# Regrouping V by TensorE for one more batch, and loading half of the first q through a second queue

## The chip, the cores and the metric

The kernel runs on one core of a Trainium2 chip. The core has a matrix engine (TensorE, PE in the profile; its weight loads are listed apart as PEld), a vector engine (VectorE, DVE), a scalar engine (ScalarE, ACT), GpSimd (POOL) and SyncE (SP), which here only issues DMAs. Each engine works through its own list of instructions in program order and waits on semaphores for the others. Matmuls write PSUM; VectorE and ScalarE copy the results out to SBUF. GpSimd's DMAs can change the type on the way (fp32 to bf16); SyncE's copy as it is.

The metric is device time in microseconds. Before the change it is 104.95 us (median of three runs, 104.95 to 105.63). The profiled execution has a span of 101.9 us from its first to its last instruction.

## The reference

Four batches, eight heads, 768 positions in eight blocks of 96, head size 64. The first half is an attention within blocks, whose keys and values are mixed over blocks by a Sinkhorn-normalized matrix P; the second half is a token mixer on the result.

```python
for _ in range(5):
    P = P - np.max(P, axis=-1, keepdims=True)
    P = np.exp(P)
    P = P / (np.sum(P, axis=-1, keepdims=True) + 1e-09)
    P = P / (np.sum(P, axis=-2, keepdims=True) + 1e-09)
k_sorted = np.einsum('bhij,bhjcd->bhicd', P, k_b)      # v_sorted likewise
scores = scale * np.matmul(q_b, k_sb.transpose(0, 1, 2, 4, 3))   # within each block of 96
attn = softmax(scores)
x = np.matmul(attn, v_sb)                    # then heads joined: (4, 768, 512)
wq = x @ w_q ; wk = x @ w_k                  # 64 columns each
W_tok = scale * np.einsum('bsd,btd->bst', wq, wk)
mixed = np.einsum('bst,btd->bsd', W_tok, x)
out = np.maximum(mixed, 0.0) @ w_out         # fp32, (4, 768, 512)
```

## The kernel before

Everything is unrolled. A string, ORDER, lists some 450 items; each has a letter for the step, a digit for the batch, a number for the part, and a last character: a PSUM bank for TensorE steps (capitals), or the engine (A ScalarE, D VectorE, P GpSimd, S SyncE) for the others. The program is written in that order, so every engine's own queue is the order of its items in the string; nothing reorders them.

The steps of a batch b:

- l: loads by GpSimd, with the cast to bf16: n = 0, 1, 2 is q, k, v of the batch (768 KB in bf16, 128 partitions by 8 heads by 6 rows by 64); l03 and l04 load the mixer's weights wqk and wo. The tiles Qn, Kn, Vn have three buffers each, so batch 3 takes those of batch 0.
- c: the Sinkhorn steps, small operations that alternate between ScalarE (Exp) and VectorE. b and B turn P and spread it to PSUM; n (VectorE for batch 0, GpSimd for the others) multiplies it by a mask into M, whose two buffers alternate by batch. i: constants (idb, the identity; zero and one fills). Z: filler matmuls on zeros while TensorE has nothing else.
- Q and q: TensorE transposes q, and the eviction writes QT. K and k: the matmul of Kn with M gives the mixed K, transposed, in KT.
- The values are needed as VT, with 96 positions of a block on partitions. There are two ways. One (F, f, A, a): the matmul of Vn with M as for K (F), an eviction to a spare tile (f), transposes on TensorE (A) and an eviction to VT (a), four parts each. The other (V, v, R): a matmul with M as the weights (V, three parts), an eviction to Vs (v), and six DMAs of 132 KB from Vs to VT that regroup partitions (R, on SyncE). Before the change batch 0 goes the first way and batches 1, 2 and 3 the second. For batch 1 there are also gates (N): GpSimd copies one element of Vs, so that later loads in its queue are not issued before the regrouping.
- S and e: scores and the Exp on ScalarE (E). P, r, x: attention times V with a row sum, reciprocal, and normalization on VectorE (X). T and t: transposes of X (XT).
- J, j, W, w, G, g, H, h: the mixer's projections and products (qkT, qD, wk, Ab, mixT), with d a copy of half of qkT to other partitions, by an engine or by a SyncE DMA. O and o: the product with wo and the eviction to ot; y: the store.

GpSimd's queue is in order: l00 l01 l02 i00 i02 l03 l11 l10 l12 n10 l04 n11 l20 n21 n20 n30, then gates N12 N11, l21, gates N12 N11 N10, l30 l22 l32 n31 l31. SyncE's begins with the load of sort_net into Pm and then has the six R of batch 1, y02, and the R of batches 2 and 3 with y00 and y01 among them, then the other stores.

The lines named in the profile are mostly those of helpers: L140 is every matmul, L144 the copy on ScalarE, L146 the copy on VectorE, L101 a load, L306 the regrouping, L322 a gate, L220 the product into M, L336 the Exp of the scores, L365 and L370 the normalization.

Of the kernel before, what the change touches and what calls it, by code (L numbers as in the profile page):

```python
# [8 lines left out]
FP32 = mybir.dt.float32  # L9
# [6 lines left out]


ORDER = """
l00P l01P l02P i00P i02P l03P c00D c01D i01D Z087 c02D i03A Z257 l11P c03D Z357 c04D Q007 Q016 l10P
Q025 c05D Z560 q02A q00A b00D B005 Z040 q01A n03D l12P n02D u00A K030 n01D n10P K022 n00D K016 l04P  # L20
k03D K004 k01A n11P k00D S050 S066 e05A k02D F014 e06A f01D F020 F032 f02A S006 f03D S014 l20P e00A
A021 F002 e01A a02D S036 n21P A010 f00D e03A S044 A031 a01D e04A n20P A007 a03D K112 a00A K104 k11D
P040 k10A P006 r04D K132 x04D P034 r00D k13A S020 x00D e02A K122 r03D Q127 x03D k12A Q116 P020 q11A
q12D T035 Q104 r02D t03A x02D P012 q10A r01D T025 x01D V120 S156 v12A t02D S122 T004 e15A T015 R14S
t00D V110 R15S t01D e12A V106 J005 n30P v10D v11A N12v N11v l21P N12v N11v N10v l30P l22P S132 l32P
J025 J014 e13A R13S j00D S110 n31P R11S J034 d00D R12S e11A W005 S102 j01D R10S S166 w00D e10A W014
d01D G005 Q221 w01A e16A S142 q22D G015 e14A Q210 g01D Q201 q21A H022 q20D H004 H016 h02A h01D l31P
h00A O043 O002 o04A O037 o00D K230 o03D K202 k23A K224 k20D P136 k22A S250 r13D S262 x13D e25A P124
e26A r12D S240 x12D P146 e24A Q303 Q312 r14D q30A x14D P110 q31D K214 T133 r11D k21A T122 x11D P106
t13A S214 t12D S220 e21A T113 r10D x10D O052 e22A V204 t11D o05A T107 v20D V220 y02S t10A V212 O016  # L30
v22A v21D R20S R21S J117 o01A R25S V320 R24S J137 R23S J106 v32D R22S j11A V302 y00S d11A W117 J126
v30A S204 R35S w11D j10D S230 R34S O027 e20A d10D R31S R30S W106 e23A V312 o02D Q325 w10D y01S v31A
K320 q32D K306 G104 k32D R32S k30A K332 R33S G114 k33D S300 g11A K316 e30A H124 k31D H112 h12A H100
h11D P226 h10A O155 r22D x22D S332 S320 O104 e33A o15A P246 P212 o10A r24D O145 x24D e32A r21D P206
x21D o14A S340 O114 y12S e34A r20D x20D T215 o11A P230 t21A S312 y10S r23D S356 T204 x23D e31A O135
e35A t20D P300 T224 o13A r30D T237 x30D t22A P312 P335 t23A J204 r31D r33D x31D J211 J224 O120 j20A
x33D d20S T304 o12A J231 W207 t30D P322 j21A y11S w20A S365 d21D W214 r32D e36A G207 x32D w21A P340
G217 r34D x34D T326 g21A T315 t32D T334 t31A H210 t33D H202 H226 h21D J305 h20A J314 h22A J325 O203
j30D J334 d30A W302 O225 o20A j31D w30D d31S G304 o22A W317 O216 w31A G314 o21A O235 g31D y20S H320
o23A H312 H306 O244 h31D y21S h30A O255 o24A O327 o25A h32D O314 y22S o32D O355 o31A y35S O337 y34S  # L40
o35A O344 y38S o33A O305 y36S o34A y37S o30A y33S
"""


# [1 line left out]
def kernel(  # L46
# [11 lines left out]
    nc = tc.nc  # L58
    B, H, S, D = q.shape
# [3 lines left out]
    P = 128  # L63
# [5 lines left out]
    DM = moe_w_out.shape[0]  # L69
# [16 lines left out]
    def tiles(name, n, shape, dtype=BF16):  # L86
        return [sb.tile(shape, dtype, name=f"{name}{i}") for i in range(n)]

    PS = psp.tile([P, 8, 512], FP32, name="ps")
# [6 lines left out]
    Qn, Kn, Vn = (tiles(n, NIN, [P, H, R6, D]) for n in ("Qn", "Kn", "Vn"))  # L96
# [3 lines left out]
    def load(t, src, b):  # L100
        nc.gpsimd.dma_start(out=t[b % NIN].rearrange("p h r d -> p h (r d)"),  # L101
                            in_=src[b].rearrange("h (p r) d -> p h (r d)", p=P))
# [12 lines left out]
    mixT = tiles("mixT", 1, [P, 2, 2, R6, P])  # L115
# [17 lines left out]
    def rows(t):  # L133
        return t.unsqueeze(2).to_broadcast([BH, NB, NB])

    def cols(t):
        return t.unsqueeze(1).to_broadcast([BH, NB, NB])
# [4 lines left out]
    def copy(e, o, i):  # L142
        if e == "A":
            nc.scalar.copy(o, i)  # L144
        else:
            nc.vector.tensor_copy(o, i)  # L146
# [2 lines left out]
        return PS[:, n, :].bitcast(BF16)  # L149


    def u_c(b, n, e):
        if n == 0:
            nc.vector.memset(Pm[:, NB:NB + 1, :], 1e-9)
            nc.vector.memset(fil, 0.0)
            nc.vector.memset(filw, 0.0)  # L156
            nc.vector.reduce_max(tmp, Pv, axis=AX.X)
            nc.vector.tensor_sub(Pv, Pv, rows(tmp))
            return
        nc.scalar.activation(Pv, Pv, ACT.Exp)  # L160
        nc.scalar.copy(filw[:, n, 0:1], fil[:, 0:1])
        nc.vector.reduce_sum(tmp, Pv, axis=AX.X)
        nc.vector.reciprocal(tmp, tmp)
        nc.vector.tensor_mul(Pv, Pv, rows(tmp))
        nc.vector.reduce_sum(tmp, Pm.rearrange("p i j -> p j i"), axis=AX.X)
        nc.vector.reciprocal(tmp, tmp)
        nc.vector.tensor_mul(Pb if n == 5 else Pv, Pv, cols(tmp))


    def u_i(b, n, e):  # L170
        if n == 0:
            nc.gpsimd.memset(idb, 0.0)
            nc.gpsimd.affine_select(out=idb, in_=idb, compare_op=ALU.not_equal, fill=1.0, base=0,
                                    pattern=[[-1, P]], channel_multiplier=1)
        elif n == 1:
            nc.vector.reduce_max(m_p, idb.rearrange("p (j s) -> p s j", s=SP), axis=AX.X)
        elif n == 3:
            nc.scalar.copy(Lx.rearrange("p i j s -> p (i j) s"),
                           idb[0:BH, 0:BH].unsqueeze(2).to_broadcast([BH, BH, SP]))
        elif n == 2:  # L180
            for t in VT:
                nc.gpsimd.memset(t.rearrange("p i (h e) -> p i h e", e=DS)[:, :, :, D:DS], 1.0)  # L182
            for t in Vs:
                nc.gpsimd.memset(t[:, :, :, D:DS], 1.0)
            for t in KT:
                nc.gpsimd.memset(t[:, :, S:S + P - BLK], 0.0)
            for t in E:
                nc.gpsimd.memset(t[:, :, 2 * TH * BLK:EW], 0.0)  # L188
                nc.gpsimd.memset(t[:, NT - 1, 2 * (NB * NP - TH * (NT - 1)) * BLK:EW], 0.0)  # L189


    def u_l(b, n, e):
        if n == 3:
            for s, w in enumerate((moe_w_q, moe_w_k)):
                nc.gpsimd.dma_start(out=wqk[:, :, s, :], in_=w.rearrange("(t p) d -> p t d", p=P))  # L195
        elif n == 4:
            nc.gpsimd.dma_start(out=wo, in_=moe_w_out.rearrange("(t p) d -> p t d", p=P))
        else:
            load((Qn, Kn, Vn)[n], (q, k, v)[n], b)

# [248 lines left out]
    def oslot(b, n):  # L449
        return ot[(b * 3 + n // 2) % NOT]  # L450

    def u_o(b, n, e, bank):
        copy(e, oslot(b, n)[:, n % 2, :], PS[:, bank, :])

    def u_y(b, n, e, bank=None):
        od = out[b].rearrange("(p r) e -> p r e", r=R6)
# [8 lines left out]
    for item in ORDER.split():  # L465
        kind, b, n, arg = item[0], int(item[1]), int(item[2:-1]), item[-1]
# [40 lines left out]
```

The softmax here doesn't subtract the row's maximum and nothing guards it: scores larger than these inputs give would overflow.

## Time and profile before

| | busy, us | share of 101.9 us |
|---|---|---|
| TensorE (PE) | 90.3 | 89% |
| weight loads (PEld) | 60.4 | 59% |
| VectorE (DVE) | 71.8 | 71% |
| ScalarE (ACT) | 73.8 | 72% |
| GpSimd (POOL) | 24.9 | 24% |
| GpSimd's DMA queue | 10.09 MB | 66.6% of 16 DMA engines |
| SyncE's DMA queue | 8.83 MB | 24.7% of 16 DMA engines |

A matmul is in the table from its start until its result is through the array, so TensorE can be shown busy while it could take more work. Busy shares are averages: the kernel has a start (Sinkhorn and first loads), a long middle and an end of products and stores, and each has its own limit. A row of groups gives the operation, what it writes and reads, the shape, the count, then busy time and the mean in ns of one, then the idle time of the engine just before it and what ended most of that. A wait is written as who waited, for whom, the total, the count and the longest.

### The profile page before, as it was taken

How to read it: one execution, taken by the hardware profiler on the slowest of the kernel's cores; microseconds unless marked ns; L12 is line 12 of the kernel's file. 1: busy time of each engine (PE TensorE's matmuls, PEld its weight loads, DVE VectorE, ACT ScalarE, POOL GpSimd, SP SyncE). 2: the span in 40 equal slices, each digit the busy share in tenths (PEclk: the TensorE clock that was granted, in tenths of full speed). 3: DMA queues.
4: the chain of work that ended last, by engine and by line, in shares of the span. 5: the costliest groups of instructions: out<-in, count | busy, mean ns of one | idle time of the engine just before them, and what ended most of it. 6: DMA issues, size and time to landing. Idle time of an engine off the chain costs nothing.

```text
span 101.9 us, 3431 instructions
## 1 busy us (share of the span) xinstructions
PE 90.3 (89%) x1468; PEld 60.4 (59%) x1468; DVE 71.8 (71%) x137; ACT 73.8 (72%) x108; POOL 24.9 (24%) x42
## 2 busy tenths in 40 slices
PE   3987897999988996968989998999999999999940
PEld 1235366888867584357968777656786865534410
DVE  3877689889994957359997777878889987046200
ACT  5231948998869999539898797979995669556650
POOL 5999459920000999100000000000000000000000
PEclk9999999999999999999999999999999999999998
DMA  0899999999999989999999999960630500055992
GB/s 3 86 205 203 203 204 187 202 210 198 204 208 204 239 118 216 237 206 203 205 204 203 253 335 315 337 214 0 278 140 0 225 6 0 19 206 206 370 344 109
DMA packets 19037, 19.12 MB, mean 188 GB/s; under 512 B 1872, under 2 KB 17104, under 8 KB 19024
## 3 DMA queue, kind: packets, MB, share of 16 engines
q0 software_dynamic: 14064, 10.09, 66.6%
q1 hardware_dynamic: 4960, 8.83, 24.7%
q8 instruction: 11, 0.18, 0.7%
q14 instruction: 2, 0.02, 0.0%
HBM read 20.19 MB, written 6.29 MB: 260 GB/s over the span
## 4 chain that ended last, share of the span: by engine, by line
DMA 43%; PE 35%; POOL 15%; issue 2%; POOLq 1%; ACT 1%
PE ps L140 35%; DMA Kn<-in_k_dram 21%; DMA Vn<-in_v_dram 19%; DMA VT<-Vs 3%; POOL Kn L101 3%; POOL Qn L101 3%; POOL M L220 2%; POOL Vn L101 2%; POOL wqk L195 1%; POOL E L189 1%; POOL gate L322 1%; POOLq L502 1%; ACT ot L144 1%; POOL E L188 0%; POOL VT L182 0%
## 5 line engine op out<-in xcount | busy, mean ns | idle before, releaser
L336 ACT ACTIVATE E<-ps 96x960 bf16<-96x960 f32 (+1 forms) x28 | 24.1, 900 | 1.8 <-PE ps L140 1.3
L140 PE MATMUL ps<-wo,mixT 128*128 128x512 bf16 x96 | 23.3, 380 | 0.9 <-ACT mixT L440 0.9
L370 DVE TENSOR_TENSOR X<-ps,R 96x896 bf16<-96x896 f32 (+1 forms) x20 | 20.0, 1003 | 0.6
L144 ACT COPY ot<-ps 128x512 f32<-128x512 f32 x20 | 11.6, 586 | 5.2 <-PE ps L140 4.6
L140 PEld LDWEIGHTS <-mixT 128*128 128x128 bf16 x96 | 8.4, 97 | 10.5 <-ACT mixT L440 1.8
L220 POOL TENSOR_TENSOR M<-PTR,m_p 128x512 bf16<-128x512 bf16 x6 | 7.9, 1316 | 14.7 <-PE ps L140 12.0
L140 PE MATMUL ps<-VT,E 96*128 96x65 bf16 x256 | 10.8, 193 | 0.1
L140 PE MATMUL ps<-fil,filw 128*128 128x512 bf16 x28 | 8.6, 455 | 2.4 <-DVE filw L156 1.6
L140 PEld LDWEIGHTS <-E 96*128 96x128 bf16 x256 | 9.3, 97 | 1.9 <-DMA VT<-Vs 0.2
L140 PE MATMUL ps<-QT,KT 64*128 64x96 bf16 x256 | 9.2, 204 | 1.0 <-ACT E L336 0.4
L144 ACT CAST KT<-ps 128x768 bf16<-128x768 f32 x8 | 6.3, 798 | 5.0 <-PE ps L140 4.9
L146 DVE CAST KT<-ps 128x768 bf16<-128x768 f32 x8 | 7.5, 954 | 2.0 <-PE ps L140 1.7
L140 PE MATMUL ps<-M,Kn 128*64 128x128 bf16 x192 | 7.4, 221 | 1.4 <-DMA Kn<-in_k_dram 1.2
L140 PEld LDWEIGHTS <-KT 64*128 64x128 bf16 x256 | 6.2, 94 | 3.4 <-issue 1.8
L140 PE MATMUL ps<-idb,X 96*128 96x96 bf16 x128 | 7.5, 206 | 0.3 <-issue 0.3
L140 PEld LDWEIGHTS <-Kn 128*64 128x64 bf16 x192 | 5.9, 109 | 3.1 <-DMA Kn<-in_k_dram 2.0
L442 DVE TENSOR_SCALAR mixT<-ps 128x1024 bf16<-128x1024 f32 x5 | 6.1, 1221 | 2.1 <-PE ps L140 2.0
L140 PEld LDWEIGHTS <-X 96*128 96x128 bf16 x128 | 6.0, 98 | 2.0 <-issue 0.9
L140 PE MATMUL ps<-idb,Qn 128*64 128x128 bf16 x192 | 6.6, 220 | 0.7 <-DMA Qn<-in_q_dram 0.7
L144 ACT COPY QT<-ps 128x1024 bf16<-128x1024 bf16 x7 | 6.9, 1009 | 0.4 <-PE ps L140 0.3
L440 ACT ACTIVATE mixT<-ps 128x1024 bf16<-128x1024 f32 x7 | 6.8, 1022 | 0.3 <-PE ps L140 0.2
L140 PE MATMUL ps<-XT,wqk 128*128 128x384 bf16 x32 | 6.9, 327 | 0.0
(75 smaller groups left out, 131.5 us busy)
## 6 DMA issues: line engine op xcount, KB each, us to landing
out_dram<-ot SPq DMA_DIRECT2D x9, 512.0 KB, 2.7
Qn<-in_q_dram POOLq DMA_DIRECT2D x4, 768.0 KB, 14.0
Kn<-in_k_dram POOLq DMA_DIRECT2D x4, 768.0 KB, 11.7
Vn<-in_v_dram POOLq DMA_DIRECT2D x4, 768.0 KB, 16.4
VT<-Vs SPq DMA_DIRECT2D x18, 132.0 KB, 4.8
out_dram<-ot SPq DMA_DIRECT2D x6, 256.0 KB, 2.1
wo<-in_moe_w_out_dram POOLq DMA_DIRECT2D x1, 512.0 KB, 17.1
qD<-qkT SPq DMA_DIRECT2D x2, 48.0 KB, 1.9
```

The lines of the kernel that those rows point to most:

```text
L101: nc.gpsimd.dma_start(out=t[b % NIN].rearrange("p h r d -> p h (r d)"), in_=src[b].rearrange("h (p r) d -> p h (r d)", p=P))
L140: nc.tensor.matmul(o, w, x, is_transpose=t, start=start, stop=stop, skip_group_check=True)
L144: nc.scalar.copy(o, i)
L146: nc.vector.tensor_copy(o, i)
L189: nc.gpsimd.memset(t[:, NT - 1, 2 * (NB * NP - TH * (NT - 1)) * BLK:EW], 0.0)
L195: nc.gpsimd.dma_start(out=wqk[:, :, s, :], in_=w.rearrange("(t p) d -> p t d", p=P))
L220: ENG[e].tensor_tensor(out=M[b % 2][:, h0:h1], in0=src.unsqueeze(2).to_broadcast([P, nh, SP, NB]), in1=m_p.unsqueeze(1).unsqueeze(3).to_br ...
L322: nc.gpsimd.tensor_copy(gate, src)
L336: nc.scalar.activation(E[b % 2][:, n, 0:2 * w * BLK].rearrange("p (t a c) -> p a t c", a=2, c=BLK), PS[0:BLK, bank:bank + 2, 0:w * BLK].re ...
L370: nc.vector.tensor_mul(xo.rearrange("p (a t d) -> p a t d", a=2, d=D), avps(bank, w)[:, :, :, 0:D], rr[b, n][:, :, 0:w].unsqueeze(3).to_br ...
L440: nc.scalar.activation(o, i, ACT.Relu)
L442: nc.vector.tensor_relu(o, i)
```

## The change

Batch 1's values go the first way too: four F, f, A, a instead of three V and v, six R and five gates. Its spare tile is mixT, which is unused at that time (batch 0 uses XT[1]). This takes regrouping DMAs away and puts matmuls and evictions in their place.

Half of the first q (four heads) is loaded by SyncE as fp32 into the same mixT, right after sort_net, and two copies on ScalarE (i04, i05) cast it into Qn; GpSimd loads the other half. An eviction of O can be split by columns over ScalarE and VectorE (engine letter B); only the very last one is.

ORDER was rewritten throughout. GpSimd's queue is now: l03, l00 (half), i00, l01, i02, l02, l12, l10, l11, l20, n10, n11, l04, l21, n21, n20, l32, l22, l31, l30, n30, n31. SyncE's is: sort_net, half of q, d00, d01, R32, R33, R20, R21, y00, R23, R22, d11, R24, R25, R35, R34, R31, y01, R30, y02, and the other stores. TensorE's, from its first Q to the first K of batch 2, is:

```
Q017 Q026 Z560 Q005 B004 Z040 K010 K022 K006 K034 S020 F002 S016 F024 F030 S042 S036 A025 A004
S050 S062 A035 F016 F110 S002 P034 A017 P040 A116 F102 P004 Q107 P020 T036 P012 A105 Q114 K136
K100 T025 T013 T002 K116 F130 Q125 J004 F122 S126 S110 A135 J024 A123 J012 S106 J032 W005 P110
S163 W012 P106 S154 G003 K120 G013 K214
```

Fillers go from 28 to 32. The code:

```diff
+    HQ = H // 2
+    stage = mixT[0].rearrange("p a c r s -> p (a c r s)").bitcast(FP32).rearrange("p (h e) -> p h e", h=HQ)
+    nc.sync.dma_start(out=stage, in_=q[0, 0:HQ].rearrange("h (p r) d -> p h (r d)", p=P))
...
+        elif n in (4, 5):
+            h = 2 * n - 8
+            copy(e, Qn[0][:, h:h + 2].rearrange("p h r d -> p h (r d)"), stage[:, h:h + 2])
...
+        elif b == 0 and n == 0:
+            nc.gpsimd.dma_start(out=Qn[0][:, HQ:H].rearrange("p h r d -> p h (r d)"),
+                                in_=q[0, HQ:H].rearrange("h (p r) d -> p h (r d)", p=P))
         else:
             load((Qn, Kn, Vn)[n], (q, k, v)[n], b)
...
-        copy(e, oslot(b, n)[:, n % 2, :], PS[:, bank, :])
+        c = 0 if e != "B" else DM // 2
+        if e == "B":
+            copy("A", oslot(b, n)[:, n % 2, 0:c], PS[:, bank, 0:c])
+        copy("D" if e == "B" else e, oslot(b, n)[:, n % 2, c:DM], PS[:, bank, c:DM])
```

More of the change, by code (lines that the diff above doesn't have):

```diff
@@ L18 @@
 ORDER = """
[L19 to L38, printed above, removed]
@@ L39 @@
-j30D J334 d30A W302 O225 o20A j31D w30D d31S G304 o22A W317 O216 w31A G314 o21A O235 g31D y20S H320
-o23A H312 H306 O244 h31D y21S h30A O255 o24A O327 o25A h32D O314 y22S o32D O355 o31A y35S O337 y34S
-o35A O344 y38S o33A O305 y36S o34A y37S o30A y33S
+l03P l00P i00P l01P i02P l02P c00D c01D i01D Z080 l12P c02D i03A Z250 l10P c03D Z350 i04A c04D Z440
+l11P i05A Q017 Q026 c05D Z560 Q005 q01A q02A b00D B004 Z040 q00A l20P n01D n02D u00A K010 n00D n10P
+K022 n03D K006 k01D k02A K034 n11P k00A k03D S020 F002 e02A S016 f00D l04P F024 e01A F030 f02D S042
@@ new lines @@
+S036 e04A f03D A025 A004 e03A a02D S050 S062 a00D A035 e05A l21P F016 a03D e06A F110 n21P f01A S002
+f11D P034 e00A A017 n20P r03D P040 x03D A116 a01A F102 r04D a11A P004 x04D l32P Q107 r00D f10A P020
+x00D q10A T036 P012 r02D A105 x02D t03A Q114 a10A K136 r01D K100 x01D k13A l22P T025 k10D q11A T013
+T002 K116 t02D t01A F130 t00D Q125 k11A J004 l31P q12D f13A F122 S126 f12A S110 A135 e12A J024 A123
+a13D J012 e11A j00D S106 a12D J032 d00S e10A W005 l30P P110 j01D S163 w00D d01S W012 r11D e16A P106
@@ new lines @@
+x11D w01A S154 G003 e15A r10D K120 x10D G013 n30P k12A K214 g01D Q212 k21A S130 q21D P146 n31P e13A
+T103 r14D S144 x14D Q202 e14A t10D H010 H006 q20D Q223 h01A h00D P124 q22A V310 r12D O022 v31D S226
+o02A O013 x12D e22A P130 o01D T112 R32S V204 r13D t11A R33S x13D V216 O003 v20A K230 v21A o00D R20S
+H024 R21S T132 k23D y00S h02A T123 R23S K206 R22S t13D K300 t12A k20D K334 O052 k30A k33D S210 o05A
+S256 S264 J113 e21A J102 e26A J133 V220 e25A j11D J122 V324 j10D d11S v22A W113 V306 w11D W102 v32A
@@ new lines @@
+O033 v30D R24S R25S S200 d10A R35S o03D K324 R34S e20A K316 R31S w10D Q313 k32D y01S k31A G102 R30S
+Q301 q31D G112 q30D Q320 g11A K224 q32D H112 k22A H106 O041 h11D h10A S234 o04D S242 e23A S316 O100
+y02S e24A P244 O131 r24D o10A x24D e31A P202 o13D S334 O110 r20D e33A x20D P216 o11A S364 H122 r21D
+O121 e36A y10S x21D h12A P234 o12A S346 r23D S302 O140 x23D e34A y11S e30A T201 o14D P224 S326 t20A
+r22D P302 x22D e32A T230 O151 r30D t23A x30D T227 o15A T216 P324 t22D y12S t21A S350 r32D P312 x32D
@@ L42 @@
+e35A J207 J216 r31D J227 x31D P340 J236 j20A P334 j21A W207 r34D d20A T313 r33D x34D W212 w20A T306
+w21A x33D G207 t30A G217 t31D T322 d21D g21A T333 t32A H200 t33D H214 H226 h20D J302 h21A J313 h22A
+J322 O225 j30D J333 d30A W302 O234 o22A j31D w30A d31A W313 G302 o23A w31D O205 y21S G312 o20A O213
+g31A H310 o21A H304 H326 h31D O252 h30A y20S O243 o25D O335 o24A h32D O322 y22S o33A O343 o32A y36S
+O357 y35S o34A O302 y37S o35A O313 y38S o30A y33S o31B y34S
 """
```

## The prediction

> **What bounds the kernel now.** The page came first, for the shares of the whole span:
>
> ```profile
> span 101.9 us, 3431 instructions
> PE 90.3 (89%) x1468; PEld 60.4 (59%) x1468; DVE 71.8 (71%) x137; ACT 73.8 (72%) x108; POOL 24.9 (24%) x42
> DMA  0899999999999989999999999960630500055992
> ```
>
> No single engine is it: TensorE looks full, DMA is full until about 65 us, VectorE and ScalarE are each over 70%. So the second view is the busy time by stage. I cut it at the first start of a few TensorE groups: K of batch 0 (13.4), V of batch 1 (29.7), K of batch 2 (44.35), K of batch 3 (61.75), the first O of batch 2 (84.7), the first O of batch 3 (92.7). The columns are length, then busy time of PE, PEld, DVE, ACT, POOL.
>
> ```profile
> 13.40:29.70 16.30, 14.73 (x369) 12.33 (x369) 14.77 (x23) 13.66 (x17) 6.92 (x6) 1.00 1.37 202
> 29.70:36.70 7.00, 6.70 (x118) 4.92 (x119) 5.09 (x10) 6.22 (x7) 3.42 (x8) 1.00 1.19 207
> 36.70:44.35 7.65, 5.98 (x91) 3.39 (x88) 4.42 (x6) 5.21 (x8) 4.47 (x5) 1.00 1.19 199
> 44.35:61.75 17.40, 16.48 (x333) 13.13 (x333) 13.97 (x23) 15.24 (x20) 0.00 (x0) 1.00 1.27 233
> 61.75:84.70 22.95, 22.76 (x399) 16.37 (x400) 19.82 (x31) 18.33 (x29) 0.00 (x0) 1.00 0.45 161
> 84.70:92.70 8.00, 8.00 (x59) 3.71 (x57) 2.96 (x5) 5.46 (x9) 0.00 (x0) 1.00 0.30 118
> ```
>
> Read the mean share of DVE and ACT: 87% in the first row (28.43 of 32.6), 63% in the third, 84% and 83% in the fourth and fifth. The PSUM evictions on these two pace the kernel as much as TensorE does, and the third row is a hole. The waits and the GpSimd timeline say why:
>
> ```profile
> POOL M L220 <- PE ps L140: 12.0, 1, 12.0
> ```
> ```profile
> 32.92 1.31 POOL L220 TENSOR_TENSOR M<-PTR,m_p 128x512 bf16<-128x512 bf16 x1 [12.00 <-PE ps L140]
> 34.64 0.94 POOL L101 DMA_DIRECT2D Kn<-in_k_dram  x1
> 44.34 1.03 PEld L140 LDWEIGHTS <-Kn 128*64 128x64 bf16 x36 [1.28 <-DMA Kn<-in_k_dram]
> ```
>
> GpSimd issues the loads in program order. It stands 12 us in n30, which overwrites the M that batch 1's V still reads, then in the gates for the regrouping; l21 (K of batch 2) is issued only at 34.6. The DMA engines run nearly dry at 37 us (37 GB/s in a quarter microsecond against a steady 203), and K of batch 2 is used at 44.35.
>
> For TensorE, busy time is too kind. I took the time from a group's first matmul to the next group's where nothing waits: O 0.865 (the last eight groups: 7.08 us), V 0.45, A 0.44, Q 0.46, G 0.44, P 0.425 (0.26 short), K and F 0.34, T 0.34, S 0.30 (0.18 short), J 0.49 and 0.165, H 0.22, W 0.21. The order's groups then sum to 73.4 us. From 44.35 to 84.7 they are 36.1 of 40.35 us (89.5%); from the first P of batch 2 (65.7) to 84.7, 17.9 of 19.0 (94%). So late in the kernel TensorE is near its issue limit.
>
> **What the Trainium skill says.** "Perfetto Trace Analysis", section "Identifying the Most-Contended Engine": matmul busy time is a poor measure, occupancy is fair for Vector and Scalar. The trace agrees: 89% busy, but 73.4 us of issue in 101.9. "DMA: Bandwidth & Descriptors", section "Issuing engines are not separate DMA queues": DMAs of all issuers share the same 16 engines, so moving half of q to SyncE saves issue time, not bandwidth; no run here shows it yet. "ScalarE: Activation LUTs", section "What ACT_TABLE_LOAD costs": neighbouring activations overlap by about 93 ns. The trace agrees: four E activations of 0.97 us take 3.55 us, 0.11 less each, so sums of row means overstate.
>
> **The change, part by part.**
> *V of batch 1.* Removed: three V groups (3 x 0.45 = 1.35 us of PE), three evictions to Vs (ACT 1.02 x 2, DVE 1.23: 3.26 us), six regrouping DMAs of 132 KB and the five gates. Added: four F (4 x 0.34) and four A (4 x 0.44), 3.1 us of PE; four f (ACT 0.80 x 3, DVE 0.95) and four a (ACT 1.01 x 2, DVE 0.69 x 2), 6.75 us. The rows of batch 0 show all of these:
>
> ```profile
> L144 ACT CAST Vs<-ps 128x1024 bf16<-128x1024 f32 x5 | 5.1, 1016 | 0.8 <-DVE X L370 0.8
> L146 DVE CAST Vs<-ps 128x1024 bf16<-128x1024 f32 x4 | 4.9, 1225 | 1.5 <-PE ps L140 1.2 <-ACT E L336 0.2
> L146 DVE CAST XT<-ps 128x768 bf16<-128x768 f32 x3 | 2.8, 946 | 0.0
> L146 DVE COPY VT<-ps 96x1024 bf16<-96x1024 bf16 x3 | 2.1, 685 | 0.3 <-ACT E L336 0.3
> L144 ACT COPY VT<-ps 96x1024 bf16<-96x1024 bf16 x1 | 1.0, 1012 | 0.0
> ```
>
> Net +1.8 us of PE and +3.5 us of eviction, 1.75 on each of ACT and DVE, on the pacing engines. The regrouping removed was 0.81 MB, some 2 us of DMA at some 400 GB/s (quarter microseconds of the regrouping and stores near 65 us show 377 to 431), and the latency from V to P (4.8 us to landing) that batch 1 no longer has.
>
> *First q by halves.* The DMA engines carry almost nothing before 4 us while GpSimd writes descriptors. SyncE, free after its 0.40 us issue of sort_net, can move 0.79 MB in this time: its fp32 half needs some 2 us at 400 GB/s, so it lands at about 5. GpSimd's stream loses 0.39 MB, 1.9 us at 203 GB/s; wqk, now ahead of it, costs 0.65 us by bytes, up to 1 for its small packets. i04 and i05 cast on ACT, 0.80 each by the 768-element rows. They add a wait in ACT's queue with the Sinkhorn Exps behind it; but i04 follows the fourth Exp (6.5) and i05 the fifth (8.3), and ACT idles 1.44 us before each later Exp. Cost nothing, hidden by DVE's Sinkhorn chain, which sets B at 12.1 and K at 13.4 as before.
>
> *Loads.* All gates go, and V1, Q1, K1, Q2, wo and K2 are queued before GpSimd waits for M of batch 0. The stream then runs without a hole at 3.87 us a load: K0 at about 11.3, V0 15.2, V1 19.0, Q1 22.9, K1 26.8, Q2 30.6, wo 33.2, K2 37.1, V3 41, V2 45, K3 48.7, Q3 52.6, the last ones up to 3 us later for stores and regrouping beside them. Before, K1 was used at 21.9, K2 at 44.35, K3 at 61.75. K1 is later, which is why F and A of batch 1 stand before it: they fill TensorE with V1.
>
> *The order.* Adding each list's evictions at the row means, the mean of ACT and DVE from the first K of batch 0 to the first K of batch 2 is 25.6 us in the old order (measured 24.7, ratio 0.965) and 23.9 in the new: 23.1. From there to the first O of batch 2 it is 36.4 old (measured 33.7, 0.926) and 39.8 new: 36.9. PE from K of batch 2 on: 36.1 old, 40.6 new, since more of batch 0 and 1 is left for later.
> First stretch at the density of the hole-free row: 23.1/0.872 = 26.5, so K of batch 2 at 39.9, after its data (37.1). Second stretch, with loads ahead of need and regrouping no longer just in time (in the chain that ended last, P of batch 2 waits 3.39 us for VT): PE at the 94% of the stretch from 65.7, 40.6/0.94 = 43.2; eviction is then at 85%, under the 87% already seen. The first O of batch 2 stands at 83.1 instead of 84.7. What follows is the same O chain (8.0 and 9.2 us). The last eviction, split over ACT and DVE, saves some 0.2 (0.59 to the 0.37 of a 256-column copy). Sum: 1.6 + 0.2 = 1.8; 104.95 - 1.8 is 103.1, and I say 103.0.
>
> *Small ones.* qD by SyncE for three halves: 1.9 us to landing against 0.26 on DVE, but H comes several groups later. SyncE's queue holds y00, waiting for an O eviction, ahead of R23, R22, d11 and the rest of R2; P of batch 2 and H of batch 1 wait for those and come 10 us of PE work later or more. l32 waits behind n20 for F of batch 0, about 21 us, with 15 us of loads still queued. Four more filler matmuls run in idle time. Cost of all: nothing.
>
> **The rivals.**
> *Denser:* without data waits, the first stretch reaches 92% and PE 96%: 13.4 + 25.1 + 42.3 = 80.8, 4.1 us gained, 100.8. For: the hole had 37% free. Against: no stretch shows 92%.
> *Eaten up:* the extra eviction and PE work take back what the hole gave: PE at 91%, 13.4 + 26.5 + 44.6 = 84.5, 104.7. For: 44.35 to 61.75 ran at 86% with loads mostly there.
> *Slower:* the hole was dependence (the H, relu, O chain, with 1.38 us waited on mixT), not loads, and comes back elsewhere: the whole stretch's 81.9% stays (116.7 of 142.6). Work 60.0/0.819 = 73.3, the O at 86.7, 2.0 later less 0.2: 106.8. For: ACT gets more than its half of the new work, and SyncE's queue can block. Against: batch 1 loses a DMA in its chain.
>
> **How the numbers follow.** Forecast 103.0: 0.45. Denser 0.25, eaten up 0.13, slower 0.17. The range takes in the denser case to just under its value and most of the slower side: 100.3 to 105.8. Below 103.9 lie the denser case and most of the forecast: 0.63. Within 1%: 0.19. Above 106.0: 0.18.
>
> **What would show it.** DMA at 203 GB/s without a dip from 4 to about 55 us; no GpSimd wait of 12 us; K of batch 2 used near 40, K of batch 3 near 50; ACT near 80 us and DVE near 72 busy; F and A of batch 1 between 19 and 28. Wrong would be the part on q if the first Q stays at 8.6 us with loads no earlier, or if ACT's Exps slip; wrong the part on density if DVE plus ACT stay under 82% from 13.4 on. A wait of PE on VT or qD of a microsecond would point to SyncE's queue.

## The result and the profile after

The changed kernel takes 104.62 us in the median (102.88 to 106.81) beside 104.95 for the kernel before. Some executions of each kernel run 1.5% or more above its fastest; the ratio compares only the others, and since the first profiled execution of the changed kernel was one of the long ones, the lines below are from a second profile of the same kernel, the run a_again. The ratio is 0.9875, 95% interval 0.9833 to 0.9918, that is 103.2 to 104.1 us on the old 104.95: a gain of 1.3 us, where the forecast of 103.0 had 1.95. In a_again the ratio is 0.9801 (0.9739 to 0.9863).

The page of the changed kernel, the lines that answer to those of before (the lines of its program have moved: L231 is the product into M, L317 the regrouping):

```profile
span 101.2 us, 3544 instructions
PE 91.7 (91%) x1528; PEld 62.1 (61%) x1528; DVE 71.5 (71%) x137; ACT 78.6 (78%) x115; POOL 23.9 (24%) x37
DMA  1899999999999999999999844952705000145992
```

The DMA line is now full from the third slice to 55 us without the dip at 37 us. ScalarE has 4.8 us more to do, TensorE 1.4 us. The stages, cut where the same groups start: K of batch 0 (13.72), K of batch 1 (28.83), K of batch 2 (39.56), K of batch 3 (52.37), the first O of batch 2 (84.0), the first O of batch 3 (91.82). Columns as before: length, then busy time of PE, PEld, DVE, ACT, POOL.

```profile
13.72:28.83 15.11, 13.38 (x337) 11.48 (x337) 13.42 (x21) 13.74 (x17) 10.38 (x10) 1.00 1.32 204
28.83:39.56 10.73, 10.56 (x232) 8.57 (x232) 7.86 (x14) 9.40 (x13) 1.64 (x2) 1.00 1.30 205
39.56:52.37 12.81, 11.70 (x224) 8.36 (x226) 10.24 (x17) 9.95 (x13) 0.97 (x1) 1.00 1.32 206
39.56:84.00 44.44, 43.33 (x791) 31.18 (x792) 36.39 (x58) 38.18 (x53) 0.97 (x1) 1.00 0.74 177
84.00:91.82 7.82, 7.82 (x59) 3.79 (x58) 3.02 (x5) 5.70 (x10) 0.00 (x0) 1.00 0.27 107
```

The mean share of VectorE and ScalarE is 90% in the first row (27.16 of 30.22) and 80% in the second; the row of 63% is gone. K of batch 2 starts at 39.56 instead of 44.35, 4.8 us earlier. Of this only 0.6 us is left at the first O of batch 2 (84.0 against 84.57), because the new order leaves more of batches 0 and 1 for later, as the forecast had it, and for a stop seen below.

The waits and the timeline of the weight loads show where the rest lies:

```profile
PEld L140 <- issue: 10.1, 29, 1.3
POOL M L231 <- PE ps L140: 13.4, 3, 6.2
```
```profile
39.56 0.36 PEld L140 LDWEIGHTS <-Kn 128*64 128x64 bf16 x12 [0.32 <-DMA Kn<-in_k_dram]
...
41.79 0.42 PEld L140 LDWEIGHTS <-Qn 128*64 128x64 bf16 x14
43.48 0.11 PEld L140 LDWEIGHTS <-Qn 128*64 128x64 bf16 x2 [1.27 <-issue]
```

GpSimd still waits 13.4 us in its products into M, but its two long waits (5.2 and 6.2 us) come when the last load is issued, at 25.7 us, and nothing is queued behind them but the next products. K of batch 2 waits 0.32 us for data. New in this length is the last line: TensorE stops in the middle of one group, Q202, after its 14th weight load, for 1.3 us. It waits for no semaphore there ("issue"), and the matmul behind it shows none either.

### The profile page after: what moved, and what is told of

Read it like the earlier page. It is cut to its first block, busy times and chain, and to the rows that moved or that the text cites. A ratio compares the mean times of both kernels' runs of the same rounds, so it can differ in the third digit from the quotient of the medians.

```text
span 102.7 us, 3533 instructions
## 1 busy us (share of the span) xinstructions
PE 92.0 (90%) x1517; PEld 62.5 (61%) x1528; DVE 71.4 (70%) x137; ACT 78.8 (77%) x115; POOL 23.9 (23%) x37
## 4 chain that ended last, share of the span: by engine, by line
PE 65%; DMA 19%; POOL 9%; issue 4%; DVE 0%; ACT 0%; POOLq 0%
PE ps L140 65%; DMA Kn<-in_k_dram 19%; POOL Vn L101 2%; POOL wqk L203 2%; POOL E L197 1%; POOL Kn L101 1%; POOL Qn L101 1%; POOL Qn L207 1%; POOL E L196 0%; DVE ot L146 0%; ACT ot L144 0%; POOL VT L190 0%; POOL idb L178 0%; POOL KT L194 0%; POOL Vs L192 0%
## 5 line engine op out<-in xcount | busy, mean ns | idle before, releaser
L140 PEld LDWEIGHTS <-mixT 128*128 128x128 bf16 (+1 forms) x128 | 10.3, 104 | 9.3 <-issue 1.2
L144 ACT COPY ot<-ps 128x512 f32<-128x512 f32 (+1 forms) x17 | 9.6, 573 | 5.2 <-PE ps L140 4.2
L140 PE MATMUL ps<-fil,filw 128*128 128x512 bf16 x31 | 10.2, 490 | 1.8 <-DVE filw L161 1.6
L231 POOL TENSOR_TENSOR M<-PTR,m_p 128x512 bf16<-128x512 bf16 x6 | 7.8, 1302 | 17.0 <-PE ps L140 14.2
L140 PE MATMUL ps<-VT,E 96*128 96x65 bf16 x256 | 11.3, 194 | 0.0
L140 PE MATMUL ps<-idb,Qn 128*64 128x128 bf16 x192 | 7.8, 221 | 1.9 <-issue 1.3
L146 DVE COPY ot<-ps 128x512 f32<-128x512 f32 (+1 forms) x8 | 5.2, 654 | 5.1 <-ACT ot L144 4.4
L140 PEld LDWEIGHTS <-Qn 128*64 128x64 bf16 x192 | 6.1, 110 | 3.7 <-issue 2.8
L144 ACT CAST KT<-ps 128x768 bf16<-128x768 f32 x9 | 7.1, 800 | 1.4 <-PE ps L140 1.4
L140 PEld LDWEIGHTS <-filw 128*128 128x128 bf16 x32 | 3.4, 118 | 7.3 <-issue 2.9
L144 ACT COPY XT<-ps 128x768 bf16<-128x768 bf16 x9 | 7.2, 805 | 0.8 <-PE ps L140 0.6
```

The costliest lines, as they stand in the source:

```text
L140: nc.tensor.matmul(o, w, x, is_transpose=t, start=start, stop=stop, skip_group_check=True)
L231: ENG[e].tensor_tensor(out=M[b % 2][:, h0:h1], in0=src.unsqueeze(2).to_broadcast([P, nh, SP, NB]), in1=m_p.unsqueeze(1).unsqueeze(3).to_br ...
```

## The experiments

The twelve runs are told by question. Where an item of the order is named, the diff is of the string ORDER.

### Is the gain there, and does the queue at the start matter?

The changed kernel again, the same with wqk behind V of batch 0 in GpSimd's queue, and the same with all of q by GpSimd:

```diff
 a_wqklate
-l03P l00P ... i02P l02P
+l00P ... i02P l02P l03P
 a_wholeq: the same, and
-i04A
-i05A
```

and in a_wholeq no half of q on SyncE.

> The changed kernel once more, for a profile beside which the others are read. If the head is late by construction[...], the first K of batch 0 starts near 14.4 us again (13.4 in the kernel before) and V of batch 0 near 18. If that was chance of one execution, the first K is back at 13.4 and V at 16 or earlier. The 1.33 and 0.74 us in which TensorE stood in the middle of a group and waited for nothing shown should sit elsewhere or be gone if they are chance. Ratio near 0.987.

> The changed kernel with one edit: the load of wqk goes behind V of batch 0 in GpSimd's queue. If the wqk descriptors ahead of q make the head late, GpSimd's half of q is issued 1.7 us earlier and lands near 8.5 instead of 10.3, the first K starts at 13.4, V of batch 0 near 17, and the kernel takes some 1 us less than the changed one (ratio to before near 0.978). If the lateness comes from elsewhere, or if the middle of the kernel has slack for it, the time stays (0.987).

> The changed kernel without the halves: all of the first q by GpSimd, first in its queue, wqk behind V of batch 0, no casts on ScalarE. If the half of q by SyncE brought anything, this is slower than the same with wqk late by up to 1.9 us of DMA stream (V of batch 0 1.9 us later, at 17 to 18), though the first K stays at 13.4, which the Sinkhorn steps set. If the order and the values' way are all that counts, it equals the kernel with wqk late, or beats the changed one by 1 us.

Measured: a_again 103.7 us (0.9801); a_wqklate 102.45 us, ratio 0.9753 (0.9706 to 0.9799); a_wholeq 104.5 us, 0.9879 (0.9784 to 0.9973). In the trace GpSimd's half of q had its last part at 8.61 us in a_again and at 7.62 in a_wqklate, V of batch 0 at 16.54 and 15.34. So wqk at the head of the queue costs a microsecond of the stream's start. The ratios are half a per cent apart and their intervals overlap, so that a gain in time isn't shown. With wqk in front the halves bring nothing that can be told from a_wholeq, which has wqk behind (0.9801 and 0.9879, overlapping); with wqk behind they may bring one per cent. And K of batch 0 starts at 13.72 in a_again and 13.82 in a_wqklate: earlier data is not what that start waits for.

### Is it the loads, or the values of batch 1?

In b_freed the kernel before keeps its old way for batch 1; the five gates go, and the loads move up.

```diff
-l20P ... n20P ... N12 N11 l21P ... N12 N11 N10 l30P l22P l32P n31P l31P
+l20P l21P ... n20P l30P l22P l32P l31P ... n31P
```

> The kernel before with its loads freed alone: the five gates are dropped, K of batch 2 is issued behind Q of batch 2, and Q3, V2, V3, K3 behind the product into M for batch 2, ahead of the one that waits 12 us. If the hole from 36.7 to 44.35 was loads, K of batch 2 is used near 40 to 41 instead of 44.3 and the kernel gains up to 2.5 us (0.976 to 0.99). If the hole was dependence (H, relu, O), or the regrouping of batch 1 now waits behind the loads and P of batch 1 comes late, the time stays or grows (1.00 to 1.02).

Measured: 103.19 us, ratio 0.9822 (0.9779 to 0.9865): the gain of the whole change, within the intervals. K of batch 2 had its last part at 42.79 us instead of 44.30, but started at 44.13 all the same, right behind the chain H, relu, O that was one of the rivals, and no longer waits for data. The gain appears later: K of batch 3 lands at 58.75 instead of 61.70 and starts at 60.94 instead of 61.75, and the first O of batch 2 stands at 83.8. K of batch 2 in b_freed, then K of batch 3 before the change and in b_freed:

```profile
44.13 0.98 PEld L140 LDWEIGHTS <-Kn 128*64 128x64 bf16 x34 [0.42 <-issue]
```
```profile
61.75 0.70 PEld L140 LDWEIGHTS <-Kn 128*64 128x64 bf16 x24 [0.44 <-DMA Kn<-in_k_dram]
```
```profile
60.94 0.73 PEld L140 LDWEIGHTS <-Kn 128*64 128x64 bf16 x24
```

So loads issued early are worth 1.8% by themselves, mostly behind batch 2, not in the hole.

The reverse, the changed kernel with the old way for batch 1 in the places of the new (chain by chain, what stands between is left out):

```diff
-F110 f11D A116 a11A   F102 f10A A105 a10A   F130 f13A A135 a13D   F122 f12A A123 a12D
+V110 v11D R12S R13S   V102 v10A R10S R11S   V120 v12A R14S R15S
```

> The changed kernel with batch 1's values the old way inside the new order: three V and v in the places of three F and f, six regrouping DMAs behind them, no A. TensorE has 1.8 us less to issue, ScalarE and VectorE 3.5 us less to evict. If the turn on TensorE earns its cost, this is slower, with P of batch 1 waiting for VT and the loads some 2 us later. If the turn is a cost that only the freed loads paid for, this is faster than the changed kernel by 1 to 2 us (ratio to before 0.965 to 0.98).

Measured: 109.4 us, ratio 1.0382 (1.0328 to 1.0437). Its waits and the chain that ended last:

```profile
PE ps L140 <- DMA VT<-Vs: 4.4, 1, 4.4
```
```profile
35.48 0.55 SPq L317
36.06 6.10 DMA VT<-Vs
```
```profile
PE   3987983999889804999999999999999999999950
PEclk9999998599999997559999999999999999999996
```

TensorE stands 4.4 us for the regrouped values: the last of six transfers takes 6.1 us beside the full stream of loads. The stand is the 0 and 4 in the middle of the PE line (38 to 43 us); from its second slice on the granted clock shows 7, 5, 5 (0.945 over the run), so part of the 5 us is clock. The trace is of an execution of 110.51 us, others took 108.05, so that its 4.4 us needn't hold for all. The places of the six R were mine, and earlier ones might have waited less; what is shown is that beside a stream that is full all along a regrouping took 6.1 us, and that in these places TensorE waited for it. In b_freed, whose stream is full too, one took 7.6 us, and TensorE's waits for VT sum to 0.2 us.

Then the turn alone, put into b_freed. In b_turn each chain F, f, A, a stands nearly back to back where a V stood:

```diff
-V120 S156 v12A ...
+F120 S156 f12A A120 a12D ...
```

> The kernel before with its loads freed and, on top, batch 1's values turned on TensorE: F, f, A, a in the places of V and v, no regrouping for batch 1. Beside the kernel with freed loads alone (0.982 of the kernel before): if the turn earns more than it costs, because P of batch 1 no longer waits for 0.81 MB of regrouping that goes beside the loads, it gains another 0.5 us or more (0.977 or less). If the turn is a pure cost once the loads are free, it adds what it puts on the evicting engines, 1 to 1.75 us (0.99 to 1.0). The first K of batch 2 is to be at 43 or later in both cases, since P of batch 1 stands behind it in this order.

Measured: 112.09 us, ratio 1.0654 (1.0601 to 1.0707); S132 at 41.8 us instead of 33.8 in b_freed. Far slower than either theory had it. In b_turn2 the chains are spread:

```diff
-F120 S156 f12A A120 a12D t02D S122 T004 e15A T015 t00D F110 ...
+F120 S156 f12A t02D S122 T004 e15A T015 t00D F110 e12A A126 f11D ...
```

> The kernel of b_turn with its four F, f, A, a chains spread out: each A stands two or three TensorE groups behind its F, with T, J and S groups of batch 0 and 1 between. Tells apart what made b_turn slow. If it was the chains standing back to back, S132 (41.8 there, 33.5 in the old order) comes back to some 35 to 36 (the turn's own 1.8 us of TensorE and 1.75 us on each of VectorE and ScalarE over the V it replaces), and the time is 103.2 (that of b_freed) to 105. If the turn itself costs more than the regrouping in this order, whatever its place, S132 stays past 38 and the time stays over 107. The six regrouping DMAs of batch 1 are gone in both, so no wait of P on VT is expected.

Measured: 108.05 us, ratio 1.0294 (1.0234 to 1.0354), S132 at 36.6. S132 lies between the two theories, the time with the second: the wider spacing took back 4 us of b_turn's 9, and the rest stays. (Part of the 4 us may be clock: the page of b_turn shows 6, 5 and 5 tenths granted between 39 and 47 us, 0.969 over the run, where b_turn2 has 0.994.) The stretch from the first group of V (29.3 us) to the first K of batch 2, in b_freed and in b_turn2:

```profile
29.30:44.13 14.83, 13.00 (x212) 8.60 (x210) 9.92 (x16) 11.98 (x15) 2.56 (x2) 1.00 1.27 222
```
```profile
29.30:49.35 20.05, 15.37 (x260) 10.53 (x260) 11.06 (x18) 13.10 (x17) 2.55 (x2) 1.00 1.31 204
```

The work grows by 2.4 us on TensorE and 1.1 us each on VectorE and ScalarE, the stretch by 5.2 us; the share of VectorE and ScalarE falls from 74% to 60%. In this place J, W, G, H and O of batch 0 follow one from the other, and an eviction put into their queues can delay the chain. So the turn is not cheap in itself. That the new order makes it so, by starting F and A of batch 1 eight microseconds earlier (21.6 to 35 us), beside the P and X of batch 0, is the likely reading, not one that a run has shown. How much of b_turn2's loss is left with still better places wasn't tried.

### The halves of q alone

```diff
 b_halfq (the kernel before)
+half of q by SyncE into mixT, i04A before c04D, i05A before Q007
```

> The kernel before with the halves of the first q alone (wqk stays where it was, behind the fills; two casts on ScalarE). If the halves are worth 1.9 us of stream, K of batch 1 is used at 20.0 instead of 21.9 and V of batch 1 at 27.8 instead of 29.3; since GpSimd's wait on V of batch 1 ends earlier too, the kernel gains 1 to 1.9 us (0.982 to 0.99). If the middle is paced by the evictions, the time stays within 0.5 us. If the casts delay the Sinkhorn steps, the first K starts later than 13.4.

Measured: 104.66 us, ratio 0.9985 (0.9956 to 1.0013): nothing. The loads did come earlier (V of batch 0 at 15.13 instead of 15.89, K of batch 1 at 19.9 instead of 20.65, medians of their parts). Some of it may have gone into a stop without a semaphore, as in the changed kernel, longer than the one at the same place before the change; here the line of before and that of b_halfq:

```profile
31.24 0.71 PEld L140 LDWEIGHTS <-X 96*128 96x128 bf16 x16 [0.53 <-issue]
```
```profile
31.53 0.71 PEld L140 LDWEIGHTS <-X 96*128 96x128 bf16 x16 [1.22 <-issue]
```

### What the stop in Q202 is

The trace lists twelve transfers of 16,384 bytes in a queue of their own, of kind "instruction". Beside the weight loads that TensorE had started by then they come one to some 127 pairs of weight load and matmul. The Trainium skill has this: "Runtime: NRT & Kernel Launch", section "Instruction fetch mechanics", says that instructions are refilled in 16 KiB blocks of 256, and that crossing a block is "mostly hidden". The size and the number agree. That it is hidden doesn't, here. In a_again the fetches start at 22.73, 28.90, 34.88, 41.09 and 47.09 us while the loads run, 6.0 to 6.2 us apart, though TensorE went through 91 to 141 pairs in between; the stop after the 734th weight load lasts from 42.1 to 43.48 (1.38 us from the start of one load to the next, 1.27 of them idle), 2.4 us after the fetch at 41.09 began.

Two kernels test it. In w_lessfill (a_wqklate with eight fillers fewer) the same count falls into another group. In w_noload the last four loads are left out: batches 2 and 3 take V, and batch 3 q and k, from what the buffers hold, so part of the result isn't computed, but all instructions of the compute engines stay.

```diff
 w_lessfill
-Z440 ... Z560
+Z520
 w_noload
-l32P l22P l31P l30P
```

> The kernel with wqk late, with eight of the 32 filler matmuls dropped (four before the first Q, four of the six between Q and B of batch 0). In all profiles of the new order TensorE stood 1.1 to 1.6 us after weight load number 734, inside a group and with no semaphore to wait for. If that is the fetch of instructions (a block ends there), it stands after number 734 again, which is now eight matmuls further in the order, in Q223 instead of Q202. If it is a wait of that group, it stays in Q202, at number 726. Dropping fillers also takes B from behind them: the first K at 13.2 to 13.4 instead of 13.8, and up to 0.6 us less in all (0.970).

> The kernel with wqk late, without the loads of Q, K and V of batch 3 and of V of batch 2; the values of batches 2 and 3 and q and k of batch 3 are taken from what the buffers hold, so that part of the result is not computed. The DMA engines are then free from 38 us on. If instruction fetch is slow because it queues behind the loads, the next fetch comes at once and the stand after number 734 shrinks from 1.6 to under 0.5 us. If it does not depend on the loads, it stays. If loads still bound the middle, the total falls by several us; if ScalarE, VectorE and TensorE pace it, by no more than the stand, 1 to 1.5 us (to about 101).

Weight loads of w_lessfill:

```profile
42.46 0.11 PEld L140 LDWEIGHTS <-Qn 128*64 128x64 bf16 x2 [0.42 <-issue]
43.55 0.44 PEld L140 LDWEIGHTS <-Qn 128*64 128x64 bf16 x14 [0.98 <-issue]
```

and of w_noload:

```profile
41.30 0.48 PEld L140 LDWEIGHTS <-Qn 128*64 128x64 bf16 x16
41.87 0.12 PEld L140 LDWEIGHTS <-Ab 64*128 64x128 bf16 x4
42.41 0.48 PEld L140 LDWEIGHTS <-Qn 128*64 128x64 bf16 x16 [0.42 <-issue]
```

With eight fillers fewer the stop is no longer in Q202 but after the second load of Q223; it is again the 734th weight load. It follows the count of instructions, not the work. The stops of the kernel before and of b_halfq come after the 480th load, 254 pairs earlier: 508 instructions, close to two blocks of 256. Without the loads the fetch comes at 37.94 instead of 40.66 (a_wqklate), and the stop is gone. w_noload takes 101.12 us (0.967, 0.964 to 0.9699) against 102.45 of a_wqklate and 102.39 of w_lessfill: 1.3 us, where the stop is 1.5 us idle in a_wqklate and 1.0 in w_lessfill. So the loads of the middle cost little more than the stop; the compute sets the pace there. Not all of the 1.3 us need be the stop's, as without the loads other transfers are faster too: SyncE's second copy to qD, which H needs, had landed at 39.44 instead of 42.80 in a_wqklate. w_lessfill takes 102.39 us (0.9788, 0.9764 to 0.9813): the fillers cost nothing measurable, though K of batch 0 starts at 13.29 instead of 13.82.

### The last eviction, and the start of K of batch 2

w_oneout is w_lessfill with the last eviction in one piece (o31A for o31B).

> The kernel with wqk late and eight fillers fewer, with the very last eviction in one piece on ScalarE. In the profiles the two halves of it run one after the other (ScalarE 0.37, then VectorE 0.42, where one piece takes 0.59): one piece should end 0.2 us earlier and the kernel take 0.2 us less (0.977 where the one with two halves had 0.979). If VectorE's half ran beside ScalarE's in other executions, one piece would cost 0.2 us.

Measured: 102.14 us, ratio 0.9703 (0.9667 to 0.974), the lowest median of the complete kernels here, 0.25 us under w_lessfill. The ends of a_again, with the split, and of w_oneout:

```profile
97.41 0.37 ACT L144 COPY ot<-ps 128x256 f32<-128x256 f32 x1 [0.28 <-PE ps L140]
97.82 0.42 DVE L146 COPY ot<-ps 128x256 f32<-128x256 f32 x1 [4.36 <-ACT ot L144]
```
```profile
96.77 0.59 ACT L144 COPY ot<-ps 128x512 f32<-128x512 f32 x1 [0.28 <-PE ps L140]
```

VectorE's half begins when ScalarE's has ended: 0.83 us from the first start to the last end, against 0.59 in one piece. The profile shows the order, not its reason (both halves read one PSUM bank and write one tile).

In a_again, a_wqklate, w_lessfill and w_noload K of batch 2 starts within 0.1 us of the landing of its last part. To see whether the loads set this start, w_k2early loads it ahead of wo, and moves one transpose into the wait for K of batch 1:

```diff
 w_k2early (w_oneout)
-l04P l21P        K136 r01D K100 x01D k13A l22P T025
+l21P l04P   T025 K136 r01D K100 x01D k13A l22P
```

> w_oneout with K of batch 2 loaded ahead of wo (the two loads change places), and the transposes T025 moved ahead of K136, where TensorE waits 0.7 us for the last pieces of K of batch 1. Tells apart what sets the start of K of batch 2 in the changed order. In all kernels of this order so far that start (39.06 to 39.56) lies within 0.1 us of the landing of the last of K's sixteen pieces. If the stream of loads sets it, its last piece now lands some 2.5 us earlier (0.5 MB at 205 GB/s), near 36.5, K214 starts at 38.5 to 38.7, half a microsecond earlier, and the time falls by 0.3 to 0.5 against w_oneout (102.14, ratio 0.970). If the evictions of the stretch set it and the landing is a coincidence, K214 stays within 0.2 of 39.1 and the time is that of w_oneout within 0.2.

Measured: the last part at 36.57 us instead of 38.99, K214 at 39.14 instead of 39.13, 102.2 us, ratio 0.973 (0.9692 to 0.9767). K214 in w_oneout and in w_k2early:

```profile
39.13 0.39 PEld L140 LDWEIGHTS <-Kn 128*64 128x64 bf16 x12
```
```profile
39.14 0.39 PEld L140 LDWEIGHTS <-Kn 128*64 128x64 bf16 x12
```

The landing was a coincidence; the stretch's own work sets the start. A wait that is new here shows how a late part can take the stop's place:

```profile
43.04 0.11 PEld L140 LDWEIGHTS <-Ab 64*128 64x128 bf16 x3 [0.97 <-DMA qD<-qkT]
```

SyncE had issued this copy to qD at 36.68; its middle part landed at 41.44, the last at 42.99. H waits for that, and the stop that would have come five weight loads later is gone. In a_again the last part of the same copy landed at 43.40, just before the stop in front of H ended (43.48): without the stop TensorE would have stood for this copy until then.

## Why the prediction was right, and where it wasn't

Its sum against the second profile of the changed kernel:

| step | forecast | measured |
|---|---|---|
| K of batch 0 | 13.4 | 13.72 |
| to K of batch 2 | 26.5 | 25.84 |
| K of batch 2 | 39.9 | 39.56 |
| to the first O of batch 2 | 43.2 | 44.44 |
| first O of batch 2 | 83.1 | 84.00 |
| from there to the end | 17.0 | 17.2 |
| span | 100.1 | 101.2 |

**The number.** It owes something to luck. The sum promises 1.8 us in the span; the two profiles differ by 0.7, of which 0.6 are there at the first O of batch 2. The same two executions took 104.28 and 102.97 us, 1.3 us apart, so the other 0.6 us lie outside the span, where the forecast had looked for nothing. It is so throughout: in the executions on record, time less span is 2.1 to 2.65 us for the kernel before, 1.74 to 1.87 for the changed kernel and its variants, some 2.1 for b_freed. The trace of before has two transfers of kind "instruction", of 8 KB, after its last instruction (at 103.73 and 104.15 us), b_freed has one, a_again none; whether they cause the difference, and what in the order sets their number, stays open.

**The hole and its density.** The stretch came out as forecast: it ran at 86% of VectorE and ScalarE (44.42 of 51.68) where 87.2% was forecast, on somewhat less work (a mean of 22.2 us instead of 23.1). The reason given for the hole was half right. With the loads freed and the old order kept, K of batch 2 still starts at 44.13, 1.3 us after its data (b_freed): the chain H, relu, O holds it. The new order filled the hole with other work, and w_k2early shows that there, too, work and not data sets the next start.

**What comes later.** The mechanism was right: more work is left behind K of batch 2, and it takes back most of the 4.8 us. The 40.6 us of issue took 44.44 us, 91.4%, where 94% was forecast. The difference is about the stop of 1.38 us for instructions: without it the share is 94.3%. In the forecast's terms the density was right and a wait was missing that no semaphore shows. The trace of before has it too (0.62 us from load to load after the 480th), and I took that for pacing. But a second term was too small at the same place: SyncE's copies to qD, put at 1.9 us to landing and at no cost, took 4.8 us in the median of a_again, and the one that landed at 43.40 would have held TensorE nearly as long. One reading of the forecast was wrong without effect on its sum: the 3.39 us for VT are the length of that DMA in the chain; TensorE waited 0.23 us for it.

**Loads.** Right in their order and without a dip; a microsecond late throughout (V of batch 0 at 16.07, K of batch 2 at 38.04 in the median, against 15.2 and 37.1), and the last part of a load another 0.9 to 1.5 us behind. The 2.8 us between K of batch 2's data and its use were used up by this, without a cost.

**The first q by halves.** Wrong, in the way that the forecast had named: its first Q starts at 9.47 us, with V of batch 0 no earlier than before (16.07 against 15.89). (The first Q didn't wait for data at the end, as its last part had landed at 8.61; it stands behind four fillers that start at 8.51.) SyncE's half landed at 6.06 instead of 5. wqk, for which the forecast allowed 0.65 to 1 us, took two issues of 0.95 and 0.76 us before GpSimd could begin on q, while the engines had little else to move, so it cost the microsecond that the half had saved. The part on ScalarE was right: no cost seen from i04 and i05. And K of batch 0 doesn't hang on q: in a_again B004 and K010 stand in TensorE's order behind Q005 and Z560, which start late:

```profile
10.49 0.98 PEld L140 LDWEIGHTS <-filw 128*128 128x128 bf16 x6
11.89 0.48 PEld L140 LDWEIGHTS <-Qn 128*64 128x64 bf16 x16 [0.42 <-issue]
12.46 0.26 PEld L140 LDWEIGHTS <-Lx 32*128 32x128 bf16 x8
```

What the Trainium skill says in "DMA: Bandwidth & Descriptors", section "Issuing engines are not separate DMA queues", fits b_halfq: with a second issuer the loads come 0.7 to 0.8 us earlier, out of the time before 4 us in which the kernel before moves almost nothing, and no faster after that.

**The last eviction.** Wrong in sign: +0.2 us instead of -0.2, as the halves run one after the other.

**The V turn.** Its work was right (ScalarE 78.6 and VectorE 71.5 us busy, near 80 and near 72 forecast), but it is no price that holds anywhere: the same four chains cost 5 us in the old order (b_turn2 against b_freed), and earned their keep only in the new order, against the places that a_v1dma gives the old way. (Its 1.75 us for each of ScalarE and VectorE is a mean: by its own list ScalarE gets 2.4 us and VectorE 1.1. And F and A of batch 1 run from 21.6 to 35 us, not from 19 to 28, as half of them stand behind K of batch 1.) The credit for the gain seems to lie with the freed loads, which bring 1.8% with neither turn, halves nor new order (b_freed). For the changed kernel itself this is argued, as no run has its order with the loads held back.

**The rivals.** "Denser" failed on the stop and the 90% of the best stretch, "slower" on the share of 86%: the dependence H, relu, O was real, as K of batch 2 in b_freed shows, but the new order put other work beside it. "Eaten up" described the direction, not the size.

## What to carry to other kernels

Undo a bundled change part by part: here the unglamorous part, loads queued ahead of a waiting instruction, brought alone as much as the whole change, while the halves of q alone measured nothing. Price an added eviction by the queue it joins, since in a stretch where each step follows from the last it delays them all. A stop inside a group of matmuls with no semaphore to name is worth looking up beside the instruction transfers. And where a gain in time is larger than the profiles' spans allow, look at what lies outside the span.

## What the hardware showed that wasn't expected

In these traces TensorE's instructions arrive as transfers of 16,384 bytes, listed among those of the core's DMA engines. While the loads keep these full, the fetches of a_again start 6.0 to 6.2 us apart; in w_noload, when its loads end, 3.7 and 4.0 us apart. A fetch brings some 127 pairs of weight load and matmul, and where TensorE goes through them faster than the next one comes, it stops: idle for 0.53 us in the kernel before, 1.22 in b_halfq, 1.27 in a_again, 1.49 in a_wqklate. One late part holds a whole load: in a_again the last of sixteen parts landed 0.2 to 0.5 us behind the median in the loads of the first 17 us, 0.9 to 1.5 us in those from 20 to 52 us and 2.1 in the last one (in the first traced execution of the changed kernel 1.8 to 2.0 in most). Whether the fetches cause this lag stays open; without its later loads, w_noload still shows it (39.02 for K of batch 2, median 38.06). And in a_v1dma and b_turn, right after TensorE had stood for microseconds, its granted clock fell to 0.5 to 0.7 for three slices of the page; the link was not tested.
